# Gating an image by its channel means: one pass under the gate of the first 220 rows, with a comparison and a second pass on chip

## The chip, the core and the metric

The kernel runs on one core of a Trainium2 chip. The metric is the device time of one execution in microseconds, the median of several runs. A core has a matrix engine (PE, TensorE), three engines for elementwise work (DVE = VectorE, ACT = ScalarE, POOL = GpSimd), and SP, which here only issues transfers. The engines share an on-chip memory of 128 partitions (SBUF) and a small accumulation memory (PSUM). 16 DMA engines move data between these and the chip's main memory (HBM); SP and ACT issue such transfers, each on a queue of its own (q1 and q10 in the profile).

## The reference

```
x: (1, 384, 384, 384) bf16 (height, width, channels), w1d: (1,) bf16
g = jnp.einsum("bhwc->bc", x) / (H * W)      # mean of each of the 384 channels
s = sigmoid(g * w1d[0])                      # one gate for each channel
return x * s[:, None, None, :]
```

x and the result have 147,456 pixels of 384 channels, 113.25 MB each. The gate of a channel depends on every pixel. The inputs are x = 0.05 times normal numbers, and one w1d that is 0.00123.

## The kernel before

A *row* below is what one row of the arena holds: 128 pixels, one on each partition, 384 bf16 each, 98,304 bytes. x has 1152 rows. The arena is the part of SBUF that holds x; it has 275 rows in the kernel before, and a tile is a run of rows that one transfer brings or takes.

The kernel goes through x twice, because the arena holds less than a quarter of it. In the first half SP loads tiles of 18, then 47 and 46 rows round the arena (`Ring`), and TensorE adds each row into one PSUM bank (`add_rows`, L213): a matmul of a matrix of ones by the row gives on every partition the sum over the 128 pixels, for all 384 channels. The tile of the first 18 rows is copied to PSUM (`parked`, L229). The last rows loaded stay in the arena (247 rows, `kept`), the last tiles being short. Then one ACT instruction makes the gate `s_bc` from the sums (L270), and the second half begins: DVE multiplies rows by the gate in place (`gate`, L280), ACT's queue stores them (`put`). First come the kept rows, in pieces of 2, 2, 4, 4, 6, ... up to 32 rows, then the parked tile, then all the other rows, which SP loads again in tiles of 48 and 47 (`load_again`).

There is no scheduler: `Planner` records for every engine a list of waits and instructions in the order in which the code calls `op` and `dma`. It derives the waits from which rows an instruction reads and writes, so an instruction waits for the last writer and the last readers of its rows, each by a semaphore. All the transfers have line L90 (`dma_start`), all of SP's waits come from there too. At the end ACT waits for every store.

Of the kernel before, what the change touches and what calls it, by code (L numbers as in the profile page):

```python
# [3 lines left out]
P = 128  # L4
ROW = 384
BF16 = mybir.dt.bfloat16
F32 = mybir.dt.float32
U32 = mybir.dt.uint32
ACT_F = mybir.ActivationFunctionType
ALU = mybir.AluOpType  # L10


class Planner:
# [6 lines left out]

    COMPUTE = ("vector", "tensor", "scalar", "gpsimd")

    def __init__(self, nc, n_dma_sems):
        self.nc = nc
        self.streams = {e: [] for e in ("sync", "scalar", "vector", "tensor", "gpsimd")}
        self.sems = {e: nc.alloc_semaphore(f"{e}_done") for e in self.COMPUTE}
        self.count = {e: 0 for e in self.COMPUTE}
        self.pool = [nc.alloc_semaphore(f"dma_{i}") for i in range(n_dma_sems)]
# [63 lines left out]
        self._record(token, reads, writes)  # L92
        return token

    def emit(self):
        with self.nc.Block() as block:
            for name, stream in self.streams.items():

                def body(e, stream=stream):
                    for kind, a, b, *c in stream:  # L100
                        if kind == "wait":
                            e.wait_ge(a, b)  # L102
                        else:
                            ins = a(e)
                            if b is not None:
                                ins.then_inc(b, c[0])

                getattr(block, name)(body)


def split(n, most):
    k = -(-n // most)
    return [n // k + (i < n % k) for i in range(k)]
# [12 lines left out]
        return self.at - n  # L126


STREAM = 48
PREFETCH = 28  # L130
RELOAD = 48
PARKED = 18
LAST_LOADS = [24, 16, 8, 4, 2]
FIRST_OUT = [2, 2, 4, 4, 6, 8, 10, 12]
OUT = 32


def bass_standalone__channel_attn_eca__vision_kernel(
# [5 lines left out]
    B, H, W, C = x.shape  # L144
    assert B == 1 and C == ROW and (B * H * W) % P == 0
    n_rows = B * H * W // P
    inv_hw = 1.0 / float(H * W)
    x_rows, o_rows = x.flatten_outer_dims(), out.flatten_outer_dims()

    def dram(view, tile, t0=0, n=None):  # L150

        r0, size = tile
        n = size if n is None else n
        whole = view[r0 * P : (r0 + size) * P, :].rearrange("(p t) c -> p (t c)", p=P)
        return whole[:, t0 * C : (t0 + n) * C]

    ones = nc.alloc_sbuf_tensor("ones", [P, P], BF16)
    s_bc = nc.alloc_sbuf_tensor("s_bc", [P, C], BF16)
    w_one = nc.alloc_sbuf_tensor("w_one", [1, 16], BF16)
    w_scaled = nc.alloc_sbuf_tensor("w_scaled", [P, 1], F32)  # L160
    warm = nc.alloc_sbuf_tensor("warm", [P, 2], F32)
    n_arena = nc.sbuf_bytes_remaining // (2 * C)
    arena = nc.alloc_sbuf_tensor("arena", [P, n_arena * C], BF16)
    parked = nc.alloc_psum_tensor("parked", [P, 7 * 512], F32)
    acc = nc.alloc_psum_tensor("acc", [P, 512], F32)
    parked_u32 = parked[:].bitcast(U32)
    parked_bf = parked[:].bitcast(BF16)
# [8 lines left out]
    plan = Planner(nc, 110)  # L176


    plan.op("gpsimd", lambda e: e.memset(warm[:, 0:1], 0.0), writes=["warm"])  # L179
# [5 lines left out]
        reads=["warm"],  # L185
        writes=["warm1"],
# [1 line left out]
    plan.op(  # L188
        "tensor",
        lambda e: e.matmul(  # L190
            acc[:, 0:1], ones[0:1, :], w_one[0:1, 0:1], start=True, stop=True
        ),
        reads=["ones", "w_one"],
        writes=["acc"],
    )
    plan.op(
        "vector",
        lambda e: e.tensor_scalar_mul(w_scaled[:], acc[:, 0:1], inv_hw),  # L198
        reads=["acc"],
        writes=["w_scaled"],  # L200
    )


    summed = [0]

    def add_rows(r0, n):
        for i in range(n):
            summed[0] += 1
            first, last = summed[0] == 1, summed[0] == n_rows
            src = at(r0 + i, 1)  # L210
            plan.op(
                "tensor",
                lambda e, src=src, first=first, last=last: e.matmul(  # L213
                    acc[:, :C], ones[:], src, start=first, stop=last
                ),
                reads=["ones"] + (rows(r0, n) if i == 0 or i == n - 1 else []),
                writes=["acc"],
                signal=i == n - 1,
            )

    n_kept = n_arena - PREFETCH
    ring = Ring(n_arena)
    done = 0
    place = ring.take(PARKED)
    plan.dma("sync", at(place, PARKED), dram(x_rows, (0, PARKED)), writes=rows(place, PARKED))
    add_rows(place, PARKED)
    plan.op(
        "vector",
        lambda e, place=place: e.tensor_copy(  # L229
            parked_u32[:, : PARKED * C // 2], at(place, PARKED).bitcast(U32)  # L230
        ),
        reads=rows(place, PARKED),
        writes=["parked"],
    )
    done = PARKED
    for n in split(n_rows - n_kept - PARKED, STREAM):
        place = ring.take(n)
        plan.dma("sync", at(place, n), dram(x_rows, (done, n)), writes=rows(place, n))
        add_rows(place, n)
        done += n  # L240


    kept = []
    sizes = []
    r = 0
    rest = n_arena - PREFETCH - sum(LAST_LOADS)
    for n in split(rest, STREAM) + LAST_LOADS:
        sizes.append((r, n))
        r += n
    gap = r  # L250
    for place, n in sizes:
        plan.dma("sync", at(place, n), dram(x_rows, (done, n)), writes=rows(place, n))
        add_rows(place, n)
        kept.append((place, n, done))
        done += n
    assert done == n_rows

    again = PARKED
    jobs = []

    def load_again(place, n):
        nonlocal again
        plan.dma("sync", at(place, n), dram(x_rows, (again, n)), writes=rows(place, n))
        jobs.append((place, n, (again, n), 0))
        again += n

    load_again(gap, PREFETCH)
    plan.op(
        "scalar",
        lambda e: e.activation(  # L270
            s_bc[:], acc[:, :C], ACT_F.Sigmoid, scale=w_scaled[:, 0:1]
        ),
        reads=["acc", "w_scaled", "warm1"],
        writes=["s_bc"],
    )


    def gate(src, dst, n):
        s_b = s_bc[:].unsqueeze(1).broadcast_to([P, n, C])
        return lambda e: e.tensor_tensor(  # L280
            dst.rearrange("p (t c) -> p t c", t=n),
            src.rearrange("p (t c) -> p t c", t=n),
            s_b,
            ALU.mult,
        )

    def put(place, n, tile, t0):
        plan.op(
            "vector",
            gate(at(place, n), at(place, n), n),  # L290
            reads=["s_bc"] + rows(place, n),
            writes=rows(place, n),
        )
        plan.final.append(
            plan.dma("scalar", dram(o_rows, tile, t0, n), at(place, n), reads=rows(place, n))
        )


    pieces = []
    first = list(FIRST_OUT)  # L300
    for place, n, r0 in kept:
        tile, t0 = (r0, n), 0
        while t0 < n:
            k = min(n - t0, first.pop(0) if first else OUT)
            pieces.append((place + t0, k, tile, t0))
            t0 += k
    for piece in pieces:
        put(*piece)


    places = Ring(n_arena)
    place = places.take(PARKED)
    plan.op(
        "vector",
        gate(parked_bf[:, : PARKED * C], at(place, PARKED), PARKED),
        reads=["s_bc", "parked"],
        writes=rows(place, PARKED),
    )
    plan.final.append(
        plan.dma(  # L320
            "scalar",
            dram(o_rows, (0, PARKED)),
            at(place, PARKED),
            reads=rows(place, PARKED),
        )
    )
    put(*jobs[0])
    for n in split(n_rows - n_kept - PARKED - PREFETCH, RELOAD):
        place = places.take(n)
        load_again(place, n)  # L330
        put(*jobs[-1])
    assert again == n_rows - n_kept
    for sem, value in plan.final:
        plan._wait("scalar", (sem, value))
    plan.emit()


# [26 lines left out]
```

## Time and profile before

| | |
|---|---|
| median of 3 runs | 744.41 us (742.28 to 747.29) |
| profiled execution, its own time | 744.33 us |
| its span, first to last instruction | 742.0 us |
| PE busy, PEld (weight loads) busy | 214.2 us, 118.3 us |
| DVE busy | 238.8 us |
| ACT busy | 2.1 us |
| HBM read, written | 200.44 MB, 113.25 MB |
| mean rate over the span | 423 GB/s |
| mean granted TensorE clock | 0.656 |

The page divides the span into 40 slices of 18.6 us. PE is busy in the first 15 of them, DVE in the remaining ones; transfers go on in all. A row of the groups names the line, the engine, the operation, output<-inputs with their shapes and the count; then the busy time, the mean of one in ns, and the idle time ahead of it with what ended that. A row of the timeline begins with the start and the duration in us.

### The profile page before, as it was taken

To read this page: it belongs to the slowest core of one execution; us is meant where nothing else is said; L and a number is where in the kernel's file an instruction comes from. 1 tells how busy PE (TensorE), PEld (TensorE's weight loads), DVE (VectorE), ACT (ScalarE), POOL (GpSimd) and SP (SyncE) were. 2 spreads that over 40 slices of the span, in tenths; PEclk is the share of its full clock that TensorE was granted. 3 is DMA by queue.
4 is the path that set the end of the run, shared out by engine and by line. 5 is a ranking of instruction groups with operands and counts; after the bars stand their busy time and mean duration, and the time that the engine had idled before them with its cause. 6 is when DMAs were issued, how large, how long until landed. Compare 5 with 4: busy or idle time off the path is not lost.

```text
span 742.0 us, 2551 instructions
## 1 busy us (share of the span) xinstructions
PE 214.2 (29%) x1153; PEld 118.3 (16%) x1153; DVE 238.8 (32%) x44; ACT 2.1 (0%) x3; POOL 0.3 (0%) x5
## 2 busy tenths in 40 slices
PE   3978787797787860000000000000000000000000
PEld 1544444454444440000000000000000000000000
DVE  2000000000000029999270234555433455543340
ACT  0000000000000000000000000000000000000000
POOL 0000000000000000000000000000000000000000
PEclk9898999999999895555555555555555555555555
DMA  9999999999999987999999999999999999999998
GB/s 381 431 428 435 435 436 431 429 431 429 427 428 432 421 357 321 411 424 426 437 418 431 413 435 437 431 433 435 434 433 427 435 438 433 429 439 429 434 436 368
DMA packets 12973, 313.86 MB, mean 423 GB/s; under 512 B 1442, under 2 KB 1954, under 8 KB 3746
## 3 DMA queue, kind: packets, MB, share of 16 engines
q1 hardware_dynamic: 7056, 200.44, 63.1%
q10 hardware_dynamic: 5906, 113.25, 35.7%
q8 instruction: 9, 0.15, 0.1%
q14 instruction: 2, 0.02, 0.0%
HBM read 200.44 MB, written 113.25 MB: 423 GB/s over the span
## 4 chain that ended last, share of the span: by engine, by line
another core or an unknown queue 42%; DMA 39%; PE 7%; DVE 5%; issue 2%; SPq 1%; ACT 0%; DVEq 0%
DMA arena<-in_x_dram 33%; PE acc L213 7%; DMA out_dram<-arena 6%; DVE arena L280 5%; SPq L90 1%; ACT s_bc L270 0%; SPq L102 0%; DVEq L102 0%
## 5 line engine op out<-in xcount | busy, mean ns | idle before, releaser
L280 DVE TENSOR_TENSOR arena<-arena,s_bc 128x18432 bf16<-128x18432 bf16 (+12 forms) x40 | 231.1, 5823 | 465.9 <-ACT s_bc L270 261.3
L213 PE MATMUL acc<-arena,ones 128*128 128x384 bf16 x1152 | 214.0, 351 | 56.2 <-DMA arena<-in_x_dram 56.2
L213 PEld LDWEIGHTS acc<-arena,ones 128*128 128x128 bf16 x1152 | 118.2, 104 | 151.7 <-DMA arena<-in_x_dram 59.1
L229 DVE COPY parked<-arena 128x3456 uint32<-128x3456 uint32 x1 | 3.8, 3761 | 5.7 <-DMA arena<-in_x_dram 5.7
L280 DVE TENSOR_TENSOR arena<-parked,s_bc 128x6912 bf16<-128x6912 bf16 x1 | 3.7, 3747 | 0.0
L270 ACT ACTIVATE s_bc<-acc,w_scaled 128x384 bf16<-128x384 f32 x1 | 0.6, 580 | 269.7 <-PE acc L213 269.7
L184 ACT ACT_TABLE_LOAD x1 | 1.3, 1283 | 1.3 <-PEq L349 1.3
L190 PE MATMUL acc<-w_one,ones 1*128 1x1 bf16 x1 | 0.2, 158 | 2.0 <-DMA w_one<-in_w1d_dram 2.0
L198 DVE TENSOR_SCALAR w_scaled<-acc 128x1 f32<-128x1 f32 x1 | 0.2, 158 | 1.2 <-PE acc L190 1.2
L180 DVE MEMSET ones<- 128x128 bf16 x1 | 0.2, 165 | 0.8 <-PEq L349 0.8
L190 PEld LDWEIGHTS acc<-w_one,ones 1*128 1x128 bf16 x1 | 0.1, 98 | 2.0 <-issue 2.0
L184 ACT ACTIVATE warm<-warm 128x1 f32<-128x1 f32 x1 | 0.2, 203 | 0.0
L349 POOL MEMSET const-bfloat16-1.0<- 128x1 bf16 x1 | 0.1, 101 | 0.0
L349 POOL MEMSET const-uint8-127<- 128x1 uint8 x1 | 0.1, 101 | 0.0
L179 POOL MEMSET warm<- 128x1 f32 x1 | 0.1, 98 | 0.3 <-POOLq L349 0.3
L349 POOL MEMSET const-float32-0.0<- 128x1 f32 x1 | 0.1, 98 | 0.2 <-issue 0.2
L349 POOL MEMSET const-float32-1.0<- 128x1 f32 x1 | 0.1, 98 | 0.0
## 6 DMA issues: line engine op xcount, KB each, us to landing
arena<-in_x_dram SPq DMA_DIRECT2D x18, 4512.0 KB, 43.6
arena<-in_x_dram SPq DMA_DIRECT2D x13, 4608.0 KB, 29.9
out_dram<-arena ACTq DMA_DIRECT2D x13, 4608.0 KB, 69.1
arena<-in_x_dram SPq DMA_DIRECT2D x6, 4416.0 KB, 44.7
out_dram<-arena ACTq DMA_DIRECT2D x5, 4512.0 KB, 50.5
out_dram<-arena ACTq DMA_DIRECT2D x4, 3072.0 KB, 24.2
arena<-in_x_dram SPq DMA_DIRECT2D x3, 3744.0 KB, 29.4
arena<-in_x_dram SPq DMA_DIRECT2D x2, 3648.0 KB, 30.2
```

The costliest lines, as they stand in the source:

```text
L90: ("op", lambda e: e.dma_start(out, in_), self.pool[i], 16)
L179: plan.op("gpsimd", lambda e: e.memset(warm[:, 0:1], 0.0), writes=["warm"])
L180: plan.op("vector", lambda e: e.memset(ones[:], 1.0), writes=["ones"])
L184: lambda e: e.activation(warm[:, 1:2], warm[:, 0:1], ACT_F.Sigmoid),
L190: lambda e: e.matmul(acc[:, 0:1], ones[0:1, :], w_one[0:1, 0:1], start=True, stop=True),
L198: lambda e: e.tensor_scalar_mul(w_scaled[:], acc[:, 0:1], inv_hw),
L213: lambda e, src=src, first=first, last=last: e.matmul(acc[:, :C], ones[:], src, start=first, stop=last),
L229: lambda e, place=place: e.tensor_copy(parked_u32[:, : PARKED * C // 2], at(place, PARKED).bitcast(U32)),
L270: lambda e: e.activation(s_bc[:], acc[:, :C], ACT_F.Sigmoid, scale=w_scaled[:, 0:1]),
L280: return lambda e: e.tensor_tensor(dst.rearrange("p (t c) -> p t c", t=n), src.rearrange("p (t c) -> p t c", t=n), s_b, ALU.mult,)
L349: nc = _bacc.Bacc("TRN2", target_bir_lowering=False, num_devices=1)
```

## The change

The kernel goes through x once. x is cut into 21 tiles of 55 rows (the last three have 54), of which the arena, now 272 rows, holds four. The sums of the first four tiles (220 rows) go to one PSUM bank, those of the other tiles to a second. After the fourth tile an early gate `s_early` is made from the 220 rows' means. Every tile is multiplied by `s_early` and stored. A load into a place waits for the store of the tile that was there. When all tiles have been summed, the full gate `s_true` is made from both sums; DVE compares the two gates bit by bit and makes a flag `redo`. SP, DVE and ACT each read the flag into a register. If it is not zero, they go through x again: load, multiply by `s_true`, store. ACT reads the flag only after all its stores have landed.

The core of the diff (the set-up of `w_scaled` for two row counts, and the removed two-pass code, are cut; `Planner.emit` now writes one engine's list where it is called):

```
+TILE = 55
+AHEAD_TILES = 4
...
+    acc = [nc.alloc_psum_tensor(f"acc{i}", [P, 512], F32) for i in range(3)]
+    def gate(place, n, s):
+        s_b = s[:].unsqueeze(1).broadcast_to([P, n, C])
+        v = at(place, n).rearrange("p (t c) -> p t c", t=n)
+        return lambda e: e.tensor_tensor(v, v, s_b, ALU.mult)
+    sizes = split(n_rows, TILE)
+    early_rows = sum(sizes[:AHEAD_TILES])
...
+    def put(place, n, r0):
+        plan.op("vector", gate(place, n, s_early),
+            reads=["s_early"] + rows(place, n), writes=rows(place, n))
+        plan.final.append(
+            plan.dma("scalar", dram(o_rows, r0, n), at(place, n), reads=rows(place, n)))
+    ring = Ring(n_arena)
+    inside = []
+    r0 = 0
+    for k, n in enumerate(sizes):
+        place = ring.take(n)
+        while inside and any(p < place + n and place < p + m for p, m, _ in inside):
+            put(*inside.pop(0))
+        load(place, n, r0)
+        inside.append((place, n, r0))
+        if k < AHEAD_TILES:
+            add_rows(place, n, 0, k == 0, k == AHEAD_TILES - 1)
+        else:
+            add_rows(place, n, 1, k == AHEAD_TILES, k == len(sizes) - 1)
+        r0 += n
+        if k == AHEAD_TILES - 1:
+            plan.op("vector", lambda e: e.tensor_copy(total[:], acc[0][:, :C]), ...)
+            plan.op("scalar", lambda e: e.activation(
+                s_early[:], total[:], ACT_F.Sigmoid, scale=w_scaled[:, 0:1]), ...)
+    for tile in inside:
+        put(*tile)
+    plan.op("vector", lambda e: e.tensor_tensor(total[:], total[:], acc[1][:, :C], ALU.add), ...)
+    plan.op("scalar", lambda e: e.activation(
+        s_true[:], total[:], ACT_F.Sigmoid, scale=w_scaled[:, 1:2]), ...)
+    plan.op("vector", lambda e: e.tensor_tensor(
+        total[:], s_true[:].bitcast(U16), s_early[:].bitcast(U16), ALU.not_equal), ...)
+    plan.op("vector", lambda e: e.reduce_max(wrong[:], total[:], axis=mybir.AxisListType.X), ...)
+    plan.op("vector", lambda e: e.tensor_copy(redo[:], wrong[:]), ...)
+    checked = (plan.sems["vector"], plan.count["vector"])
...
+        def second_pass(name, e):
+            e.wait_ge(*checked)
+            flag = e.value_load(redo[0:1, 0:1], min_val=0, max_val=1)
+            with e.If(flag > 0):
+                if name != "scalar":
+                    e.wait_ge(stored, 1)
+                again.emit(name, e)
...
+        @block.scalar
+        def _(e):
+            plan.emit("scalar", e)
+            for token in plan.final:
+                e.wait_ge(*token)
+            e.sem_inc(stored, 1)
+            second_pass("scalar", e)
```

Two places show what the engines now do in turn. The first is SP, the queue of loads, where in the kernel before the last tiles of the first half and the first reloads stand (a wait for `dma_` is one for a transfer, here for stores of the pieces that lie in the place):

```order
L90 DMA arena<-in_x_dram 128x768
L90 DMA arena<-in_x_dram 128x10752
L90 DMA arena<-in_x_dram 128x18432 [waits dma_39,dma_38,dma_40,dma_37,vector_done]
L90 DMA arena<-in_x_dram 128x18432 [waits dma_42,dma_43,dma_41,vector_done]
L90 DMA arena<-in_x_dram 128x18432 [waits dma_45,dma_46,dma_44,vector_done]
```

And SP in the changed kernel, from its first load to the fourth place's second tile, and then the end of its list (21120 elements are 55 rows; `a_dma_5` is the first tile's store, `a_dma_7` the second's):

```order
L91 DMA arena<-in_x_dram 128x21120 x4
L91 DMA arena<-in_x_dram 128x21120 [waits a_dma_5,a_vector]
L91 DMA arena<-in_x_dram 128x21120 [waits a_dma_7,a_vector]
L91 DMA arena<-in_x_dram 128x21120 [waits a_dma_9,a_vector]
L91 DMA arena<-in_x_dram 128x21120 [waits a_dma_11,a_vector]
...
L91 DMA arena<-in_x_dram 128x20736 [waits a_dma_35,a_vector]
L91 DMA arena<-in_x_dram 128x20736
L326 TENSOR_LOAD redo [waits a_vector]
```

Four loads have nothing to wait for; from the fifth on each waits for the store of one tile. The last load has no wait of its own, since it goes to the rows behind the fourth place and the two that it shares with an older tile are free by then. All reloads are gone from this list, except those behind the branch.

The second place is DVE, where the first gates stand. In the kernel before, they come behind the whole sum (`scalar_done` is the gate), in growing pieces:

```order
L229 COPY parked<-arena 128x3456 [waits dma_1]
L280 TENSOR_TENSOR arena<-arena,s_bc 128x768 [waits tensor_done,dma_21,scalar_done]
L280 TENSOR_TENSOR arena<-arena,s_bc 128x768
L280 TENSOR_TENSOR arena<-arena,s_bc 128x1536 x2
L280 TENSOR_TENSOR arena<-arena,s_bc 128x2304
```

In the changed kernel they are whole tiles, the first behind the copy of the first bank and the early gate (`a_scalar`), and the fifth and later ones each behind its own tile's load and sum (`a_tensor`):

```order
L249 COPY total<-acc0 128x384 [waits a_tensor]
L165 TENSOR_TENSOR arena<-arena,s_early 128x21120 [waits a_dma_1,a_scalar]
L165 TENSOR_TENSOR arena<-arena,s_early 128x21120 [waits a_dma_2]
L165 TENSOR_TENSOR arena<-arena,s_early 128x21120 [waits a_dma_3]
L165 TENSOR_TENSOR arena<-arena,s_early 128x21120 [waits a_dma_4]
L165 TENSOR_TENSOR arena<-arena,s_early 128x21120 [waits a_tensor,a_dma_6]
```

The multiplications have moved from behind the last row's sum to behind the 220th row's, and a tile's sum now stands between its load and its multiplication.

More of the change, by code (lines that the diff above doesn't have):

```diff
@@ L7 @@
 F32 = mybir.dt.float32
[L8 removed]
+U16 = mybir.dt.uint16
+I32 = mybir.dt.int32
 ACT_F = mybir.ActivationFunctionType
@@ L190, in bass_standalone__channel_attn_eca__vision_kernel @@
         lambda e: e.matmul(
-            acc[:, 0:1], ones[0:1, :], w_one[0:1, 0:1], start=True, stop=True
+            acc[2][:, 0:1], ones[0:1, :], w_one[0:1, 0:1], start=True, stop=True
         ),
         reads=["ones", "w_one"],
-        writes=["acc"],
+        writes=["acc2"],
+    )
+    for i, n in enumerate((early_rows, n_rows)):
+        plan.op(
+            "vector",
+            lambda e, i=i, n=n: e.tensor_scalar_mul(
+                w_scaled[:, i : i + 1], acc[2][:, 0:1], 1.0 / float(P * n)
+            ),
+            reads=["acc2"],
+            writes=[f"w_scaled{i}"],
+        )
@@ new lines, in load, with add_rows @@
+    def load(place, n, r0):
+        plan.dma("sync", at(place, n), dram(x_rows, r0, n), writes=rows(place, n))
+    def add_rows(place, n, bank, first, last):
+        for i in range(n):
+            plan.op(
+                "tensor",
+                lambda e, i=i: e.matmul(
+                    acc[bank][:, :C],
+                    ones[:],
+                    at(place + i, 1),
+                    start=first and i == 0,
+                    stop=last and i == n - 1,
+                ),
+                reads=["ones"] + (rows(place, n) if i in (0, n - 1) else []),
+                writes=[f"acc{bank}"],
+                signal=i == n - 1,
+            )
@@ L221, in bass_standalone__channel_attn_eca__vision_kernel @@
[L221 to L226, printed above, removed]
+        lambda e: e.tensor_tensor(
+            total[:], s_true[:].bitcast(U16), s_early[:].bitcast(U16), ALU.not_equal
+        ),
+        reads=["s_true", "s_early"],
+        writes=["total"],
+    )
     plan.op(
         "vector",
[L229 to L233, printed above, removed]
-    )
@@ L256, in bass_standalone__channel_attn_eca__vision_kernel @@
[L256 to L275, printed above, removed]
@@ L278, in gate @@
[L278 to L288, printed above, removed]
+        lambda e: e.reduce_max(wrong[:], total[:], axis=mybir.AxisListType.X),
+        reads=["total"],
+        writes=["wrong"],
+    )
+    plan.op(
+        "vector",
+        lambda e: e.tensor_copy(redo[:], wrong[:]),
+        reads=["wrong"],
+        writes=["redo"],
+    )
@@ L289, in put @@
+    checked = (plan.sems["vector"], plan.count["vector"])
+    again = Planner(nc, "b", 50)
+    ring = Ring(n_arena)
+    r0 = 0
+    for n in sizes:
+        place = ring.take(n)
+        again.dma("sync", at(place, n), dram(x_rows, r0, n), writes=rows(place, n))
+        again.op(
             "vector",
-            gate(at(place, n), at(place, n), n),
-            reads=["s_bc"] + rows(place, n),
+            gate(place, n, s_true),
+            reads=rows(place, n),
             writes=rows(place, n),
@@ L293, in put @@
         )
-        plan.final.append(
-            plan.dma("scalar", dram(o_rows, tile, t0, n), at(place, n), reads=rows(place, n))
-        )
[L299 to L331, printed above, removed]
```

154 lines of the change are left out of this document (79 added, 75 removed).

## The prediction

> **What bounds the kernel now.** I read the page's slices and queues first, then the chain of waits, then busy time by stretches. In the slices, DMA is the share of time in which the 16 engines move data:
>
> ```profile
> span 742.0 us, 2551 instructions
> DMA  9999999999999987999999999999999999999998
> GB/s 381 431 428 435 435 436 431 429 431 429 427 428 432 421 357 321 411 424 426 437 418 431 413 435 437 431 433 435 434 433 427 435 438 433 429 439 429 434 436 368
> HBM read 200.44 MB, written 113.25 MB: 423 GB/s over the span
> another core or an unknown queue 42%; DMA 39%; PE 7%; DVE 5%; issue 2%; SPq 1%; ACT 0%; DVEq 0%
> ```
>
> The transfers are never idle for long except in slices 15 and 16, and the chain's largest named share is DMA; its 42% of "unknown queue" lies between the moments at which SP may issue another reload, so it is transfers too. 200.44 MB are read, although x has only 113.25 MB (as many as are written): the difference, 87.2 MB, is x read twice. Stretches of the span tell whether the rate depends on the mix (columns after the time: PE, PEld, DVE, ACT, POOL busy, granted clock, DMA share, GB/s):
>
> ```profile
> 20.00:255.00 235.00, 190.36 (x1039) 105.67 (x1037) 0.00 (x0) 0.00 (x0) 0.00 (x0) 0.92 1.00 430
> 256.00:273.00 17.00, 16.47 (x92) 9.28 (x89) 0.00 (x0) 0.49 (x1) 0.00 (x0) 0.90 0.95 397
> 273.00:318.00 45.00, 0.00 (x0) 0.00 (x0) 44.88 (x18) 0.09 (x1) 0.00 (x0) 0.54 0.87 350
> 360.00:700.00 340.00, 0.00 (x0) 0.00 (x0) 145.57 (x15) 0.00 (x0) 0.00 (x0) 0.50 1.00 432
> 703.00:738.00 35.00, 0.00 (x0) 0.00 (x0) 9.53 (x1) 0.00 (x0) 0.00 (x0) 0.50 1.01 435
> 738.00:739.00 1.00, 0.00 (x0) 0.00 (x0) 0.00 (x0) 0.00 (x0) 0.00 (x0) 0.50 0.67 289
> 739.00:742.00 3.00, 0.00 (x0) 0.00 (x0) 0.00 (x0) 0.00 (x0) 0.00 (x0) 0.50 0.17 72
> ```
>
> Loads alone run at 430 GB/s, loads and stores together at 432, stores alone at 435. So a byte costs the same wherever it goes; the time is bytes over about 432 GB/s, plus the stretches in which nothing can be moved.
>
> **What the change removes and moves.** The changed kernel reads x once and writes it once: 2 x 113.25 = 226.5 MB, 87.2 MB less; at 432 GB/s that is 202 us. Against this stands one stop, because the gate of a tile now has to wait for 220 rows and the arena takes no fifth tile. I build the new span from its start.
>
> **1. The first four loads.** In the trace of before, the tiles after the first have 47 rows, and the sum of each starts when it has landed:
>
> ```profile
> 18.82 10.25 PE L213 MATMUL acc<-arena,ones 128*128 128x384 bf16 x47 [4.90 <-DMA arena<-in_x_dram]
> 29.54 7.81 PE L213 MATMUL acc<-arena,ones 128*128 128x384 bf16 x47 [0.47 <-DMA arena<-in_x_dram]
> 40.74 9.49 PE L213 MATMUL acc<-arena,ones 128*128 128x384 bf16 x47 [3.38 <-DMA arena<-in_x_dram]
> 51.45 7.81 PE L213 MATMUL acc<-arena,ones 128*128 128x384 bf16 x47 [1.22 <-DMA arena<-in_x_dram]
> 62.15 1.14 PE L213 MATMUL acc<-arena,ones 128*128 128x384 bf16 x3 [2.89 <-DMA arena<-in_x_dram]
> ...
> 19.12 0.15 PEld L213 LDWEIGHTS acc<-arena,ones 128*128 128x128 bf16 x1 [0.17 <-issue]
> 19.44 0.15 PEld L213 LDWEIGHTS acc<-arena,ones 128*128 128x128 bf16 x1 [0.17 <-issue]
> ```
>
> At 18.82 us 18 + 47 = 65 rows are there, at 62.15 us 253: 43.33 us for 188 rows, 0.2305 us a row. So 220 rows are there at 18.82 + 155 x 0.2305 = **54.5 us**.
>
> **2. The stop.** Nothing can be loaded until a store frees a place, and no store can start before the early gate. The last tile's 55 sums: 47 took 7.81 us after a short idle time and 9.49 us after 3.38 us; here PE idles some 2 to 3.5 us between tiles (12.7 us of loading less 9 to 11 of summing), so I take the slow row: 9.49 + 8 x 7.81/47 = 10.8 us (9.1 by the other). Then copy, sigmoid and the first gate:
>
> ```profile
> L229 DVE COPY parked<-arena 128x3456 uint32<-128x3456 uint32 x1 | 3.8, 3761 | 5.7 <-DMA arena<-in_x_dram 5.7
> L270 ACT ACTIVATE s_bc<-acc,w_scaled 128x384 bf16<-128x384 f32 x1 | 0.6, 580 | 269.7 <-PE acc L213 269.7
> L280 DVE TENSOR_TENSOR arena<-arena,s_bc 128x18432 bf16<-128x18432 bf16 x13 | 126.8, 9756 | 145.3 <-DMA arena<-in_x_dram 145.3
> L280 DVE TENSOR_TENSOR arena<-arena,s_bc 128x18048 bf16<-128x18048 bf16 x5 | 47.8, 9558 | 59.4 <-DMA arena<-in_x_dram 59.4
> out_dram<-arena ACTq DMA_DIRECT2D x3, 192.0 KB, 2.2
> ```
>
> The copy of 384 fp32 from PSUM: 384/3456 of 3.76 us, 0.4 us. The sigmoid 0.6. The gate of 55 rows: 0.516 ns an element (198 ns for 384), 9.756 + 2688 x 0.516 ns = 11.1 us; of 54 rows 10.9. A small store takes 2.2 us to land, of which its 192 KB are 0.45 at 435 GB/s; so 1.75 us pass beside the data, and I put all of it ahead of the first byte (between 0 and 2.2). The sum: 54.5 + 10.8 + 0.4 + 0.6 + 11.1 + 1.75 = **79.2 us**; for 24.7 us nothing is moved. The old kernel hid its gate behind stores of 2 rows first; here a whole tile is gated before its store. That is the price of the change.
>
> **3. From there on.** 226.49 - 21.63 = 204.87 MB remain (220 rows are 21.63 MB). At 432 GB/s they take 474.2 us if the engines always have something: 79.2 + 474.2 = **553.4 us**. Do they? A load of tile k+4 waits for the store of tile k; a store waits for load, sum and gate. In the old second half the same pairing ran with five places of 48 rows:
>
> ```profile
> SPq L102 <- DMA out_dram<-arena: 439.1, 23, 57.9
> arena<-in_x_dram SPq DMA_DIRECT2D x13, 4608.0 KB, 29.9
> out_dram<-arena ACTq DMA_DIRECT2D x13, 4608.0 KB, 69.1
> ```
>
> SP waited for stores 439.1 us and yet the DMA share was 1.00. A pair of 4608 KB takes 9.44 MB/432 = 21.8 us; the load's 29.9 us are about 22 at half the rate and 8 behind its forerunner; the stores' 69.1 us mean that some three were queued. In the new loop a pair of 55 rows takes 10.81 MB/432 = 25.0 us, so four places give a tile 100 us for its round. It needs 25 (load at half rate) + 11.5 (sum) + 11.1 (gate) + 25 (store) + twice 1.75 = 76 us. 24 us are left, in which a store waits in its queue: about one store is always ready, and the engines do not run dry. If TensorE stayed slow throughout (the first rows of the tile of 18.82 us came every 0.32 us, 19.12 to 19.44), the sum would take 17.6 us and 18 us would be left: still covered. DVE is busy 11.1 of 25 us, PE 11.5: neither bounds.
>
> **4. The end.** When the last load lands, most of one store (10.4 us) and a whole one (12.4) are left to move: 22.8 us. Meanwhile the last tile needs its sum (10.25 + 7 x 0.166 = 11.4 us, the row after the longest idle time), its gate 10.9 and 1.75: 24.1. I count 1.3 us of gap (0 to 7, the latter with slow sums). The last rows of the stretches above show how the old span closes: from 738 us on 0.51 MB were left (289 GB/s for one microsecond, 72 for three), 1.2 us at 435 GB/s, but the span ended 4.0 us later: 2.8 us for the engines' uneven ends and the closing. 553.4 + 1.3 + 2.8 = 557.5.
>
> **5. The comparison.** Four DVE instructions and a sigmoid on 384 columns, behind the last gate on DVE: each is like the 0.58 us row, some 2 us, beside the last store's 12.4 us. SP and DVE then read the flag at their own time. ACT alone reads it after the last store has landed: a load of a register and a branch, which no row of before shows. The nearest small read is that of w1d, issued at 0.72 us and waited for by this row until 2.04 us:
>
> ```profile
> L190 PE MATMUL acc<-w_one,ones 1*128 1x1 bf16 x1 | 0.2, 158 | 2.0 <-DMA w_one<-in_w1d_dram 2.0
> q8 instruction: 9, 0.15, 0.1%
> ```
>
> That is 1.3 us, which I take; between 0 and 5 (three such round trips, and a fetch of code behind the branch; code came in 9 packets). 557.5 + 1.3 = **558.8 us** of span. The Trainium skill ("DMA: Bandwidth & Descriptors", Latency and other measured facts) gives a floor of about 600 ns for such a register load, and "Advanced Engine Details and Errata" (Control Flow Timing) about 108 ns for compare-and-branch: by that estimate it would be 0.7 us and the span 558.2; no trace of before shows either. "Runtime: NRT & Kernel Launch" (Instruction fetch mechanics) adds that a taken branch out of the fetched window stalls for a fetch; its price is not given, and nothing here shows one.
>
> The profiled execution took 744.33 us with a span of 742.0: 2.3 us lie outside, and it is within 0.1 of the runs' median of 744.41. 558.8 + 2.3 = **561 us**, 183 less than before (202 saved in bytes, some 19 lost in the stop and the exit).
>
> **Bounds.** Low: the fast sum (-1.7), nothing ahead of the first byte (-1.75), 435 GB/s (-3.3), no gap (-1.3), no price of the flag (-1.3): 552. High: the loads' 0.2305 us a row is 426.5 GB/s, which gives +6.1; a late start +0.5; slow sums at the end +6; the flag +4: 578.
>
> **Rivals.** *The ring runs dry.* One load in flight and one store behind it is less than before had: the next load is issued only when a store has landed. If the store behind it isn't ready then, 1.75 us show for each of the 17 later tiles: 30 us, 591; if both hand-offs show, 60 us, 621. Against it: the 24 us of slack above, and DMA at 1.00 before. It decides when sum and gate together take over 46 us (100 less two transfers and both hand-offs; 22.6 by the rows). 10%.
>
> *The rate falls.* In the stretch from 273 to 318 us, with DVE busy throughout and small stores, only 350 GB/s went: 204.87 MB would take 585 us, 672 in all. Against it: that stretch had a hole and small pieces; 55-row transfers are larger than the 48-row ones at 432. 3%. The Trainium skill ("DMA: Bandwidth & Descriptors", Where 436 GB/s comes from) says that between HBM and SBUF a core's share of about 358 GB/s binds; by that estimate 572 us, 659 in all. The trace disagrees, at 432 over 340 us in both directions.
>
> *The second pass runs.* One of 384 columns whose two gates differ as bf16 suffices. Then everything is read and written again behind the last store: 226.5 MB/432 = 524 us and some 6 of head and end, **1091 us**, far slower than before. The reference's inputs speak against it: w1d is 0.00123, the mean of any channel times it is at most 1.7e-6 over 28,160 pixels, so each exact gate is within 4.2e-7 of 0.5, while bf16's neighbours of 0.5 are 0.4980 and 0.5039. It would take a sigmoid that jumps right at zero. 2%.
>
> *The stores don't start early* (the change doesn't do what it says): the order of DVE shows the first gate behind the copy of acc0 alone, so I give it under 1%.
>
> **Chances.** Forecast within 552 to 578: 80%; dry ring 10%; other ends of small terms 5%; rate 3%; second pass 2%. The range reaches a little into the dry ring: 552 to 582. A change under 1% is about what can't be told from none; all cases but the second pass lie far beyond that: faster 97%, within 1% 1%, slower 2%.
>
> **What would show it.** In the profile after: 113.25 MB read; DMA idle from about 54 to 79 us, and the first gate of 11.1 us starting near 66; loads every 25 us and a DMA share of 1.00 up to the end; no instruction that reads s_true but the comparison. A DMA share of 0.95 in the middle is the dry ring; a full share with fewer GB/s is the rate; 226 MB read is the second pass. Most fragile are the length of the stop and the half-and-half sharing of load and store.

## The result, and the profile after

The changed kernel takes **562.41 us** (median of 4 runs, 561.89 to 564.19) against 743.87 us for the kernel before in the same group of runs: a ratio of 0.756, 95% interval 0.7529 to 0.7592. The forecast was 561. The profiled execution took 564.19 us with a span of 562.4.

The head of its page, the slices of DMA, and the queues of loads (q1) and stores (q10):

```profile
span 562.4 us, 2470 instructions
DMA  9996059999999999999999999999999999999947
GB/s 379 433 431 297 1 240 388 430 433 427 433 433 434 433 433 436 431 433 430 433 431 436 436 436 439 437 433 433 431 433 430 437 429 438 431 429 429 438 204 332
q1 hardware_dynamic: 3024, 113.25, 46.9%
q10 hardware_dynamic: 3026, 113.25, 46.8%
HBM read 113.25 MB, written 113.25 MB: 403 GB/s over the span
```

x is read once. There are two dips instead of the old one: a deep one in slices 3 to 5 (the stop) and one in slice 38 (the end); between them the rate is the old 432. The flag was not set: 226.5 MB in all leave no room for a second pass. PE in order of time (start, duration, tile by tile) shows the stop and the rhythm:

```profile
41.97 11.88 PE L206 MATMUL acc<-arena,ones 128*128 128x384 bf16 x55 [4.09 <-DMA arena<-in_x_dram]
54.47 9.11 PE L206 MATMUL acc<-arena,ones 128*128 128x384 bf16 x55 [0.62 <-DMA arena<-in_x_dram]
122.17 11.05 PE L206 MATMUL acc<-arena,ones 128*128 128x384 bf16 x55 [58.59 <-DMA arena<-in_x_dram]
...
523.08 11.80 PE L206 MATMUL acc<-arena,ones 128*128 128x384 bf16 x54 [14.14 <-DMA arena<-in_x_dram]
```

The fourth tile is there at 54.47 us (forecast: 54.5). From the fifth to the last, 16 tiles follow in 400.9 us, 25.06 us a tile (forecast: 25.0). DVE and ACT at the stop, and DVE at the end:

```profile
63.62 0.56 DVE L249 COPY total<-acc 128x384 f32<-128x384 f32 x1 [61.15 <-PE acc L206]
64.21 0.61 ACT L255 ACTIVATE s_early<-total,w_scaled 128x384 bf16<-128x384 f32 x1 [61.43 <-DVE total L249]
64.86 44.36 DVE L165 TENSOR_TENSOR arena<-arena,s_early 128x21120 bf16<-128x21120 bf16 x4 [0.68 <-ACT s_early L255]
76.05 470.27 ACTq L91 DMA_DIRECT2D out_dram<-arena  x21
...
534.99 10.96 DVE L165 TENSOR_TENSOR arena<-arena,s_early 128x20736 bf16<-128x20736 bf16 x1 [14.99 <-PE acc L206]
```

The first store is issued at 76.05 us. The last gate starts at 534.99 and takes 11 us. What was moved meanwhile stands in these stretches (the last two columns are DMA share and GB/s):

```profile
66.00:70.00 4.00, 0.00 (x0) 0.00 (x0) 4.00 (x1) 0.00 (x0) 0.00 (x0) 0.76 0.00 0
140.00:500.00 360.00, 161.48 (x774) 85.70 (x775) 160.51 (x15) 0.00 (x0) 0.00 (x0) 0.70 1.00 433
535.00:540.00 5.00, 0.00 (x0) 0.00 (x0) 5.00 (x1) 0.00 (x0) 0.00 (x0) 0.92 0.82 357
540.00:545.00 5.00, 0.00 (x0) 0.00 (x0) 5.00 (x1) 0.00 (x0) 0.00 (x0) 0.50 0.02 8
```

A reading hint: this view books a packet where it starts, and a packet here takes 1.56 us, so data seem to end early by that. From the transfers' own records in the same trace: no data moved from 53.99 to 76.93 us (22.9 us; one fetch of code at 61 us aside) and from 542.56 to 546.83 us (4.3 us); the last byte went at 560.17 us, the last store landed at 560.64, and the span ended at 562.38.

### The profile page after: what moved, and what is told of

It reads as the page before. It is cut to its first block, busy times and chain, and to the rows that moved or that the text cites. A ratio compares the mean times of both kernels' runs of the same rounds, so it can differ in the third digit from the quotient of the medians.

```text
span 562.4 us, 2470 instructions
## 1 busy us (share of the span) xinstructions
PE 234.6 (42%) x1153; PEld 125.7 (22%) x1153; DVE 236.1 (42%) x29; ACT 2.7 (0%) x4; POOL 0.3 (0%) x5
## 3 DMA queue, kind: packets, MB, share of 16 engines
q1 hardware_dynamic: 3024, 113.25, 46.9%
q10 hardware_dynamic: 3026, 113.25, 46.8%
HBM read 113.25 MB, written 113.25 MB: 403 GB/s over the span
## 4 chain that ended last, share of the span: by engine, by line
DMA 62%; DVE 14%; PE 14%; another core or an unknown queue 7%; issue 0%; ACT 0%; SPq 0%; DVEq 0%
DMA arena<-in_x_dram 32%; DMA out_dram<-arena 30%; DVE arena L165 14%; PE acc L206 14%; SPq L91 0%; ACT s_true L273 0%; ACT s_early L255 0%; DVE total L281 0%; DVE total L249 0%; DVE wrong L289 0%; DVE total L267 0%; DVE redo L295 0%; SPq L99 0%; DVEq L99 0%
## 5 line engine op out<-in xcount | busy, mean ns | idle before, releaser
L206 PE MATMUL acc<-arena,ones 128*128 128x384 bf16 x1152 | 234.5, 374 | 298.2 <-DMA arena<-in_x_dram 298.2
L165 DVE TENSOR_TENSOR arena<-arena,s_early 128x21120 bf16<-128x21120 bf16 (+1 forms) x21 | 233.5, 11129 | 248.3 <-PE acc L206 247.6
L206 PEld LDWEIGHTS acc<-arena,ones 128*128 128x128 bf16 x1152 | 125.6, 111 | 406.8 <-DMA arena<-in_x_dram 306.0
## 6 DMA issues: line engine op xcount, KB each, us to landing
arena<-in_x_dram SPq DMA_DIRECT2D x18, 5280.0 KB, 34.2
out_dram<-arena ACTq DMA_DIRECT2D x18, 5280.0 KB, 42.9
out_dram<-arena ACTq DMA_DIRECT2D x3, 5184.0 KB, 22.9
```

What stands on the lines that cost most here:

```text
L165: return lambda e: e.tensor_tensor(v, v, s_b, ALU.mult)
L206: lambda e, i=i: e.matmul(acc[bank][:, :C], ones[:], at(place + i, 1), start=first and i == 0, stop=last and i == n - 1,),
```

## The experiments

The times of before were 743.87 to 744.91 us in the groups with several rounds. The changed kernel, run again in the second group, took 563.51 us.

> The changed kernel as it is, to compare with the others of this group on one chip: 562 us within 1.

### Is the stop the full arena waiting for the gate?

```
-AHEAD_TILES = 4
+AHEAD_TILES = 2
```

> The early gate comes from 2 tiles (110 rows) instead of 4; the comparison and the second pass stay. Theory (the stop is the full arena waiting for the gate): the gate is then ready while the third and fourth tile still load, the first store follows the last of the four loads without a break, and the 22 us without transfers (54 to 76 us) vanish: 540 us, DMA share 0.9 or more in every stretch up to the end. Rival (the stop is the turn from loads to stores itself, or the delay comes back later since all else is bound as before): the break only moves, 555 us or more.

Measured: **540.60 us** (ratio 0.7246, 0.7215 to 0.7277).

```profile
37.73 0.56 DVE L249 COPY total<-acc 128x384 f32<-128x384 f32 x1 [35.25 <-PE acc L206]
...
50.00:54.00 4.00, 4.00 (x27) 2.39 (x25) 4.00 (x2) 0.00 (x0) 0.00 (x0) 1.00 0.93 391
54.00:60.00 6.00, 3.16 (x16) 1.56 (x15) 6.00 (x1) 0.00 (x0) 0.00 (x0) 0.89 0.94 408
80.00:500.00 420.00, 181.68 (x878) 96.70 (x878) 181.47 (x17) 0.00 (x0) 0.00 (x0) 0.70 1.00 432
```

The copy stands at 37.73 us instead of 63.62, and the stretches around 54 us, empty in the changed kernel, carry 391 and 408 GB/s. The 22 us are gained, and hardly anything gives them back (the gap before the last store is 6.0 us here, 4.3 in the changed kernel): the stop is shown to be the early gate coming later than the arena is full.

A second edit leaves the early gate at four tiles and gates and stores the first tile in pieces:

```
+        for m in (3, 5, 9, 15, n - 32) if r0 == 0 else (n,):
             plan.op("vector", gate(place + t0, m, s_early), ...)
```

> As the changed kernel with its early gate from four tiles, but the first tile is gated and stored in pieces of 3, 5, 9, 15 and 23 rows. Theory (11.2 us of the stop are the gating of a whole first tile): the first store starts after 0.75 us of gating instead of 11.2, some 10 us earlier, and the pieces follow each other fast enough (a row is gated in 0.20 us and stored in 0.23): 552 us. Rival (the next load waits for all pieces, and small stores move data slower, so most of it is lost again): 558 us or more.

Measured: **556.50 us** (0.7474, 0.7445 to 0.7502), 7 us less than the changed kernel in the same group; between theory and rival.

```profile
65.16 44.64 DVE L165 TENSOR_TENSOR arena<-arena,s_early 128x1152 bf16<-128x1152 bf16 x8 [0.68 <-ACT s_early L262]
118.42 11.16 DVE L165 TENSOR_TENSOR arena<-arena,s_early 128x21120 bf16<-128x21120 bf16 x1 [8.62 <-PE acc L206]
...
70.00:75.00 5.00, 0.00 (x0) 0.00 (x0) 5.00 (x2) 0.00 (x0) 0.00 (x0) 0.50 0.82 340
75.00:80.00 5.00, 0.00 (x0) 0.00 (x0) 5.00 (x2) 0.00 (x0) 0.00 (x0) 0.50 0.79 334
```

By the records the first store's data start at 66.83 us, 10.1 earlier, as expected. But then stores alone move at 334 to 340 GB/s where some 430 would be possible: between the pieces the records show four gaps without data of 0.5 to 1.4 us, 3.8 us together. The 10 us are gained and 3 lost again to stores that wait for a gate one after the other; the next tile is still gated whole.

### Do four places keep the transfers fed, and how close is it?

```
-    ring = Ring(n_arena)
+    ring = Ring(3 * TILE)        # and AHEAD_TILES = 3
```

> The arena is used for three tiles only, and the early gate comes from three tiles. Theory (a tile's round needs about 76 to 80 us of load at half rate, sum, gate, store and hand-offs, and three places give 75): the ring is just dry: DMA share some 0.93 to 0.98 in the middle, 570 to 590 us; the stop is as long as before (22 us), 13 us earlier. Rival (a lone transfer runs at full rate, so the round shrinks to fit and three places do as well as four): within 3 us of 562.

Measured: **588.81 us** (0.7900, 0.7873 to 0.7928).

```profile
100.00:500.00 400.00, 171.84 (x841) 91.92 (x842) 167.38 (x15) 0.00 (x0) 0.00 (x0) 0.69 0.99 416
566.00:570.00 4.00, 0.00 (x0) 0.00 (x0) 4.00 (x1) 0.00 (x0) 0.00 (x0) 0.81 0.00 0
arena<-in_x_dram SPq DMA_DIRECT2D x18, 5280.0 KB, 28.0
out_dram<-arena ACTq DMA_DIRECT2D x18, 5280.0 KB, 27.0
```

The time is what the ring's sum gave, but not by the sign that I named: the DMA share stays at 0.99 and the rate falls, to 416 GB/s (433 in the changed kernel). The queues show what is gone: from issue to landing a load takes 28.0 us and a store 27.0, only 2 to 3 us more than the 25 of a tile at half rate, so hardly anything waits in a queue any more. With four places they take

```profile
arena<-in_x_dram SPq DMA_DIRECT2D x18, 5280.0 KB, 34.2
out_dram<-arena ACTq DMA_DIRECT2D x18, 5280.0 KB, 42.9
```

34.2 and 42.9, that is 77 us against 55: 22 us of a round are spent in queues, which is the slack that the prediction put at 24. The records also show why the share stays up: it counts the time of packets, and the packets take longer. Of the loads' 42 KB packets between 100 and 500 us, 269 of 2003 take over 1.7 us with three places, 19 of 2051 with four; their mean is 1.65 us against 1.56. What holds a packet up so long is not shown.

The medians are 26 us apart, the two profiled spans 29 (591.6 and 562.4). Of these 29, 9 are the end (with no store queued, 13.5 us pass without data before the last store, against 4.3), nearly 2 a longer stop (24.6 us against 22.9), and 18 the lower rate.

### Is it the bytes?

Both edits below read part of x again, about as many bytes as the change took away, without using them.

```
         load(place, n, r0)
+        if k > AHEAD_TILES:
+            load(place, n, r0)
```

> Each of the 16 tiles behind the fifth is loaded twice into its place (the second load waits for the first), 86.2 MB more to read, about as many as the change took away. Theory (time is bytes over 432 GB/s while a transfer is always ready): 199 us more, 761 us, DMA share 1.00 in the middle. Rival (a good part of the gain came from the order: no turn with small pieces, no second half that waits for the first): clearly less than 190 us more. If the doubled loads' hand-offs show: over 780 us.

Measured: **839.50 us** (1.1272, 1.1218 to 1.1325): 77 us more than its bytes.

```profile
HBM read 199.46 MB, written 113.25 MB: 372 GB/s over the span
SPq L91 <- DMA arena<-in_x_dram: 650.4, 16, 44.0
125.00:780.00 655.00, 176.74 (x872) 94.83 (x870) 176.13 (x16) 0.00 (x0) 0.00 (x0) 0.63 0.95 390
```

SP waits 650.4 us, 16 times, for the first load of a pair, and whatever is behind it in SP's list waits too. So the queue of loads is empty at each of these hand-offs; the rate falls to 390. This run can't answer the question: it adds a wait as well as bytes. The next one loads into rows that no tile uses:

```
         load(place, n, r0)
+        if AHEAD_TILES <= k < len(sizes) - 1:
+            load(4 * TILE, 52, r0)
```

> Beside each load from the fifth to the twentieth tile, 52 rows of x are loaded once more into arena rows that no tile uses: 81.8 MB more to read, and nothing of the tiles waits for them. Theory (time is bytes over 432 GB/s while a transfer is always ready; the doubled loads of the earlier run lost 77 us beyond their bytes because each tile had two landings one after the other): 189 us more, 752 us, 430 GB/s in the middle. Rival (the read of 86 MB more is dearer than its bytes, because loads and stores are no longer paired): 780 us or more.

Measured: **775.41 us** (1.0419, 1.0372 to 1.0466), 212 to 213 more than the changed kernel, where the bytes alone give 189; between theory and rival.

```profile
HBM read 195.04 MB, written 113.25 MB: 397 GB/s over the span
200.00:600.00 400.00, 123.36 (x605) 65.92 (x605) 118.28 (x11) 0.00 (x0) 0.00 (x0) 0.64 1.00 429
740.00:750.00 10.00, 9.29 (x48) 4.93 (x46) 0.61 (x1) 0.00 (x0) 0.00 (x0) 0.85 0.03 10
750.00:760.00 10.00, 0.00 (x0) 0.00 (x0) 10.00 (x1) 0.00 (x0) 0.00 (x0) 0.67 0.00 0
```

In the middle a byte costs what it did within 1%, at two loads to one store too: 429 GB/s. The profiled span is 214 us longer than that of the changed kernel, 25 beyond the bytes. Most of this lies at the end, where the loads come last and the stores are out: 19.3 us without data before the last store, 15 more than in the changed kernel. The other 10 are a lower mean rate from the first store to that gap, 423 GB/s against 428.6, with a first gap of 1.3 us at 713 us in it. So with about as many bytes (308.3 against 313.7 MB) the new order, with the reads put in this way, is 4% slower than the old one: the gain is the bytes, and the stop and the end are its price.

### What would the second pass cost, and what does the flag?

```
-            total[:], s_true[:].bitcast(U16), s_early[:].bitcast(U16), ALU.not_equal
+            total[:], s_true[:].bitcast(U16), s_early[:].bitcast(U16), ALU.is_equal
```

> The comparison asks for equal instead of not equal, so the flag is set and the second pass runs. Theory (bytes at 432 GB/s, loads first, no sum in the round and no stop): the first pass's 560 us and then some 4 us of head, 524 us of transfers and about 6 us of end: 1095 us, 226.5 MB read; a fetch of the second pass's code would show as a gap of some us ahead of its first load. Rival (without the sums in the round the second pass is quicker, or slower because loads and stores pair up otherwise): off by more than 15 us from 1095.

Measured: **1093.52 us** (one run).

```profile
HBM read 226.49 MB, written 226.49 MB: 415 GB/s over the span
557.62 132.26 SPq L91 DMA_DIRECT2D arena<-in_x_dram  x8
572.96 11.16 DVE L165 TENSOR_TENSOR arena<-arena,s_true 128x21120 bf16<-128x21120 bf16 x1 [26.73 <-DMA arena<-in_x_dram]
```

The rival of 1091 us was priced right. SP issues the second pass's first load at 557.62 us, 0.16 us after the last store's landing (557.46), and its tile is there 15.3 us later, as in the first pass (issue at 0.74, sum at 16.28): no wait for code shows in the time. A fetch is not excluded by that, since SP had passed its branch at 547.69 us, while the last store was still on its way.

Three runs on the flag. The first leaves out the reading of the flag and the second pass; the second reads it nine times on ACT; the third keeps the reading and the branch, but leaves out the second pass, so that the branch skips a single wait.

> The gates are compared and the flag is made, but no engine reads it and no second pass follows. Theory (reading the flag behind the last store costs about 2 us; the changed kernel's span ended 4.2 us behind the last data, that of the kernel before 2.0 us): 2.2 us less, 560.2 us, the span ending some 2 us behind the last data. Rival (the closing is that of any program with these transfers, the flag costs nothing): same time within 0.3 us.

> As the changed kernel, but ACT reads the flag nine times instead of once behind its last store. Theory (one read of the flag from on-chip memory into a register costs most of the 2.2 us by which the changed kernel ends later behind its last data): 12 to 16 us more, 575 us. Rival (the 2.2 us are the branch and what follows it, a read is cheap): less than 5 us more.

> As the changed kernel, with the flag read and the branch in SP, DVE and ACT, but the code that the branch skips is a single wait instead of the whole second pass. Eight more reads of the flag had moved the end by some 4 us, 0.5 us each, so 1.7 of the 2.2 us are not the read. Theory (they are the jump over the second pass's code): the span ends some 2.6 to 2.9 us behind the last data, as against 4.2. Rival (the branch itself or what the program's end adds to it): 4.0 us or more as before. The time is 561 to 563 us in both.

Measured: 560.82 us (0.7526, 0.7504 to 0.7547), 567.24 us and 560.96 us (one run each). The 2.2 and 4.2 us of these expectations came from the view of stretches, which books packets at their start; with the records they have to be corrected:

```
                          last store landed   span ended   between
the kernel before              741.57           742.05      0.48 us
the changed kernel             560.64           562.38      1.74
flag not read                  560.48           560.90      0.42
flag read nine times           559.53           565.45      5.92
branch over one wait           557.83           559.17      1.34
```

So the flag costs 1.74 - 0.42 = 1.3 us: the first run's theory had the sign right and the size (2.2) not. Eight more reads add 4.2 us, 0.52 each, so the second run's rival held, a read is cheap. In ACT's records the first read takes 0.49 us, a repeated one 0.27, the register work behind it 0.15 to 0.17 and the branch 0.05. The third run's theory, 1.3 to 1.6 us less, failed: it ends 0.4 us earlier. From the branch to the next instruction behind the skipped code 0.43 us pass in the changed kernel, 0.12 where the branch skips one wait. The 0.3 us between them are not a price of the distance, though: ACT with nine reads jumps over the same second pass in 0.12 us, and has instead a pause of 0.34 us in the register work behind its eighth read, where the others have 0.03. What this pause is stays open. The Trainium skill ("Runtime: NRT & Kernel Launch", Instruction fetch mechanics) says that a taken branch out of the fetched window waits for a fetch. Whether the jump here leaves that window no run shows; such a wait has at most these 0.3 us here. The medians of the runs can't show 1.3 us across groups.

### The end, and a better version

```
+LAST = [28, 14, 7, 3]            # then [28, 24]; AHEAD_TILES = 2
-    sizes = split(n_rows, TILE)
+    sizes = split(n_rows - sum(LAST), TILE) + LAST
```

> Early gate from two tiles as in the earlier run (540.6 us), and the last 52 rows come in tiles of 28, 14, 7 and 3 instead of the end of 54-row tiles. Theory (at the end the last tile's landing, sum, gate and start, 25 us, outlast the stores that are left, so that some 8 us pass without transfers): with a last tile of 3 rows its sum and gate take some 2 us, the stores are never out: 532 to 534 us, no stretch without transfers ahead of the last landing. Rival (small last tiles cost as much in hand-offs as they save): 538 us or more.

> Early gate from two tiles, and the last 52 rows as tiles of 28 and 24. Theory (tiles of 14, 7 and 3 rows loaded slowly beside stores with larger pieces; a last tile of 24 rows needs some 13 us from landing to store, and 15 us of stores are then left): no stretch without transfers and no slow tail: 532 to 534 us. Rival (the end is bound by the last landing as before, or the small tiles were no loss): 536 us or as the earlier 535.7.

Measured: **535.67 us** (0.7204, 0.7171 to 0.7236) and **534.54 us** (0.7175, 0.7161 to 0.7189). The 6.0 us without any data that the records show ahead of the last store in the version with 54-row tiles at its end (540.60 us) are gone in both (0.3 us are left in the second), and the times lie 1.7 and 0.5 us above the range that both theories gave. But the ends are not full. The second version's profile is of an execution that took 540.40 us, 5.9 more than the median, so its end need not be that of the others. In it only one to three of the 16 engines still have something to move from 523.5 to 530 us, packets of the last store but one; the others have run out:

```profile
525.00:530.00 5.00, 0.00 (x0) 0.00 (x0) 5.00 (x2) 0.00 (x0) 0.00 (x0) 0.99 0.12 52
```

So, in that execution, its rival is half right: the way of the last tile from landing to store still ends later than most of the other stores. This version, with an early gate of 110 rows, the comparison and the second pass, has the lowest median found. The first one's end in PE's order:

```profile
494.70 6.39 PE L207 MATMUL acc<-arena,ones 128*128 128x384 bf16 x28 [7.18 <-DMA arena<-in_x_dram]
510.31 4.66 PE L207 MATMUL acc<-arena,ones 128*128 128x384 bf16 x14 [9.22 <-DMA arena<-in_x_dram]
522.11 2.42 PE L207 MATMUL acc<-arena,ones 128*128 128x384 bf16 x7 [7.13 <-DMA arena<-in_x_dram]
528.01 1.14 PE L207 MATMUL acc<-arena,ones 128*128 128x384 bf16 x3 [3.48 <-DMA arena<-in_x_dram]
```

14 rows take 15.6 us after the 28, and 7 rows another 11.8, though a row costs 0.23 us of transfer. While the stores still had their 42 KB packets, from 495 to 515 us, the records have 310 packets of loads with 1.9 MB beside 163 packets of stores with 6.6 MB. So the small load tiles got far fewer bytes through beside the large stores. Whether that costs anything against two tiles of 28 and 24 rows stays open: the intervals of the two versions overlap.

## Why the prediction was right, step by step

| | forecast | measured (span of the changed kernel) |
|---|---|---|
| 220 rows loaded | 54.5 us | 54.47 |
| last sum, copy, sigmoid, gate of 55 rows | 10.8 + 0.4 + 0.6 + 11.1 | 9.11 + 0.56 + 0.61 + 11.16 |
| first byte of a store | 79.2 | 76.93 |
| from there to the end of the last but one store | 461.9 us | 465.6 |
| gap before the last store | 1.3 | 4.3 |
| last store | 12.3 | 13.3 |
| from its last byte to the span's end, with the flag | 4.1 | 2.2 |
| span | 558.8 | 562.4 |

The forecast of 461.9 us is 199.56 MB (all but 220 loaded rows and the last tile's store) at 432 GB/s.

**The main term**, 87.2 MB less at 432 GB/s, held: 433 GB/s in the middle, 113.25 MB read, and 429 GB/s when other bytes were put back beside it.

**The stop** was right in place and cause (the run with two tiles), and 2.3 us too long. Its sum ran at the fast row's pace (9.11 us after 0.62 us of idle time, where I had taken the slow row), and a store's first byte came 0.9 us after the gate, not 1.75. The pace differs between executions: in the run without the flag's reading the same sum took 10.79 us after 2.01 us of idle time, and no data moved for 24.6 us. The other part of a small store's time lies behind its data: the last store landed 0.5 us after its last byte.

**The ring** held, with the slack that was worked out (22 us against 24), and it is not a wide margin: with one place fewer 26 us are lost. The sign that I had named for it (a falling DMA share) was wrong: the rate falls, the share doesn't. By the signs of the prediction, three places would have been taken for the rival of a lower rate.

**The long stretch** took 3.7 us more than its bytes at 432 GB/s. By the records, 2.5 of them lie at its close, where the engines end one after the other (8.19 MB took 21.4 us from 521.14 us on, 19.0 at 432 GB/s), and 1.6 from 90 to 100 us, where the loads start up beside the stores (3.61 MB, 8.4 us at 432 GB/s). The forecast had counted uneven ends only behind the last store.

**The end** was mis-sized: 4.3 us of gap, not 1.3 (3.1 in the profile of the changed kernel run again). The last tile's way was right: 23.75 us from its sum's start at 523.08 to its store's first byte at 546.83, forecast 24.1. The step that failed is what the stores still have to move when the last load lands. The forecast put it at 22.8 us; by the records 7.35 MB were left at 523.08 us, 17.0 us at 432 GB/s, which the engines' uneven end stretched to 19.5. One part is the landing, which the forecast counted as the moment of the last byte: the last load's bytes end at 521.14 us, 1.9 us ahead of its sum. The other is that even then only 8.19 MB were left, 19.0 us at 432 GB/s: the stores were 3.8 us further ahead of the loads. One start of this is in the records, and the forecast put nothing on it: the fifth tile's load is issued at 90.08 us and its first byte moves at 95.0, behind packets of the store already under way. That this alone makes up the 3.8 us is not shown.

**Behind the last byte** the forecast had 2.8 us for uneven ends and the closing. It took them from the view that books a packet where it starts, which made the old span seem to end late. By the records the kernel before ended 0.8 us behind its last byte (741.24 to 742.05), and the changed one without the flag 0.8 too (560.11 to 560.90). The uneven end lies ahead of the last byte, in the last store's 13.3 us instead of 12.3.

**The flag** cost 1.3 us, the number of the forecast, by luck. The row of w1d that stood for it is a transfer from HBM; what was paid is a read of on-chip memory with its register work and branch (0.82 us) and the jump behind it.

**The rivals**: the dry ring, the lower rate and the second pass did not come; the first and the last were made to come, at 588.8 (with three places) and 1093.5 us. The second pass had been put at 1091. The dry ring had been put at 591 to 621 by hand-offs of 30 to 60 us, while the profiled span lost 18 us in rate and 9 at the end; that the times come out so near is in part chance.

The errors partly cancelled (-2.3 at the stop, +3.7 in the long stretch, +3.0 and +1.0 at the end, -1.9 behind it), to +3.6 in the profiled span. That execution was also the slowest of the four, 1.8 us above the median, and 1.8 us rather than 2.3 lay outside its span. So 561 against 562.41 is closer than the terms are, and partly luck.

## What to carry to other kernels

Where the transfer engines are busy throughout, count bytes first, at the rate that the trace shows for the same mix, and then list the stretches in which nothing *can* be moved: here a full arena that waits for a decision, and the last tile's way from landing to store. Decide as early as the arena still has something to load: the same kernel with the gate from 110 rows instead of 220 lost the stop entirely. It pays where the two gates agree, as they do for these inputs; with the second pass the kernel takes 1093.5 us, far more than the 744 of before. To judge whether n buffers are enough, add up one buffer's round, with both transfers at half rate, and compare it with n times the bytes' time; what is left over showed up here, with four places, as queueing time between issue and landing.

## What the runs showed of the hardware that was not expected

- Two queues with packets of one size got equal shares, 21.67 and 21.58 MB between 200 and 300 us where both had 42 KB packets; where the loads had packets of 2 to 11 KB beside the stores' larger ones it was 1.9 against 6.6 MB. The small side had more packets (310 against 163) and far fewer bytes, so neither count was shared evenly; the rule behind it was not taken apart.
- A load's landing is 0.5 us behind its last byte when it is alone (53.99 to 54.47 us) and 1.9 us beside stores (521.14 to 523.08). In the records the transfer's own closing packets of 4 bytes tell where the difference lies: the last of them is over with the data when the load is alone (54.00 us), and starts 1.5 us behind the data beside stores (522.67 us), about one 1.56 us packet later. That a packet of the other queue stands in between is my reading; no run took it apart.
- A read of the flag into a register took 1.05 us on SP and 1.13 on DVE while the last store was moving (changed kernel), 0.47 and 0.55 in the version with the last tile of 3 rows, where both read behind the last landing.
- The DMA share can stay at 0.99 while the rate falls by 4%; GB/s is the better sign. The share counts a packet's time, and with three places the packets of loads took 1.65 us instead of 1.56.
- The 16 engines don't end together: in the changed kernel 11 of them were still moving data at 539.5 us, 6 at 540.5, one at 541.5 and 542.5. A gap begins for most of them before it begins for all.
